# Two biases of a top-k softmax: a column on VectorE and a column on POOL, or both columns in one POOL product

## Chip, core and metric

The kernel runs on one core of a Trainium2 chip. The metric is the device time of one execution in microseconds (us), the median of several runs.

## What is computed

The reference is a chain of three layers. Of the first, the lines that matter here are these:

```python
top_k = 32
scores = scale * np.matmul(q, k.transpose(0, 1, 3, 2))
kth = np.partition(scores, -top_k, axis=-1)[..., -top_k:-top_k + 1]
scores = np.where(scores >= kth, scores, -1000000000.0)
scores = scores - np.max(scores, axis=-1, keepdims=True)
attn = np.exp(scores)
attn = attn / (np.sum(attn, axis=-1, keepdims=True) + 1e-09)
out = np.matmul(attn, v)
```

There are 4 batches, 8 heads, 576 positions and a head width of 64. Two mixture layers follow: `(x @ w_a) * (x @ w_b) @ w_out` on the 2304 tokens, then a router that picks one of 8 experts for each token, and that expert's two matrix products. Everything is float32.

## The kernel before

**The attention loop** runs over 144 rows. A "row" is 128 query positions against 576 keys, a tile `s` of 128x576. Rows are grouped in 32 parts; a part is a pair of heads with 256 or 320 of its query positions, and has 4 or 5 rows. One turn of the loop is one step. In a step, each row in flight is at another stage:

- Two steps ahead, TensorE (PE) makes the scores in PSUM (L359) and ScalarE (ACT) copies them to `s` in two halves (L360).
- `topk` (VectorE, DVE) finds the 32nd largest value of each line: four MAX8 (L380), each giving eight values of the tile `t` of 128x32, and three MATCH_REPLACE8 (L383) that blot out what was found. Each of the latter has a MATCH_VALUE_LOAD ahead of it, which reads the eight values of the MAX8. Two rows are interleaved: in one step DVE does the second half of the older row and the first half of the newer.
- Behind the older row's last MAX8 (and behind one MAX8 of the newer row) stands L385: the threshold, column 31 of `t`, times 2^66, into column 1 of a small tile `bi`.
- Two steps later, `softmax`: ACT makes a penalty, Relu(2^66 * (threshold - s)), with column 1 of `bi` as its bias (L392, called the Relu below). POOL then negates the row's largest value, column 0 of `t`, into column 0 of `bi` (L394) and subtracts the penalty from `s` (L395, the subtraction). At the start of the next step, ACT takes the exponential with column 0 of `bi` as its bias (L397).
- One step after that, PE transposes the result (L414), ACT copies it out (L417), and PE multiplies it by `v` (L453) at the end of a part.
- At a part's end `finish` runs on POOL: a product (L465) and a split in two halves (L216, L217). It is emitted at the end of a step.

Around this, POOL and ACT also convert the weights of the next layer (L531, L539, L541) up to about the fortieth row, and PE does the next layer's products between the rows (L672, L641), with POOL making two small products for each piece (L681, L628). The router of that layer has a short chain through all engines; in it ACT's L731 reads DVE's L729.

**What sets the order.** In this loop the order on PE, DVE, ACT and POOL is the order in which the code emits the instructions. Each engine works through its own list in order, and waits when an operand is not there. The DMA queue on SP is ordered by the scheduler. What follows the loop (from about 867 us) is the rest of the second layer and then the experts, and there only PE's order is written by hand.

The step's emission around the change is this: first the exponential of the row before, then a new `softmax` for row step-2, then sums of a part, then the step's share of `topk`; later, after the step's first transposes and scores, the Relu, and after the next transposes the subtraction.

```python
            with tc.high_priority(offset=FG):
                next(soft, None)
                soft = softmax(live[step - 2]) if 0 <= step - 2 < NRW else none
```

Of the kernel before, what the change touches and what calls it, by code (L numbers as in the profile page):

```python
# [10 lines left out]
F32 = mybir.dt.float32  # L11
# [6 lines left out]
OP = mybir.AluOpType  # L18
# [3 lines left out]
HUGE = float(2.0 ** 66)  # L22
# [60 lines left out]
def fused_kernel(  # L83
# [18 lines left out]
    pe, dve, act, pool, sp = nc.tensor, nc.vector, nc.scalar, nc.gpsimd, nc.sync  # L102
# [3 lines left out]
    P = 128  # L106
# [10 lines left out]
    cst = ctx.enter_context(tc.tile_pool(name="cst", bufs=1))  # L117
# [44 lines left out]
    dve.memset(eps, 1e-9)  # L162
    half = cst.tile([P, 1], F32, name="half")
    dve.memset(half, 0.5)

    tau1 = cst.tile([P, 1], F32, name="tau1")

# [28 lines left out]
    with ExitStack() as ph:  # L196
# [166 lines left out]
        def topk(t, fold):  # L363


            H2 = S // 2
            t.bi = wk.tile([P, 2], F32, name="bi", bufs=6)
            y = wk.tile([P, S], F32, name="y", bufs=YB)

            t8 = wk.tile([P, 32], F32, name="t8", bufs=6)  # L370
            t.top, t.thr = t8[:, 0:1], t8[:, 31:32]
            if fold:
                dve.tensor_tensor(y[:, :H2], t.s[:, :H2], t.s[:, H2:], op=OP.max)
                dve.tensor_tensor(y[:, H2:], t.s[:, :H2], t.s[:, H2:], op=OP.min)
                views = [(y[:, :H2], y[:, :H2])] * 2 + [(y, y)] * 2
            else:
                views = [(t.s, y)] + [(y, y)] * 3
            for r, (cur, rest) in enumerate(views):
                v = t8[:, r * 8 : r * 8 + 8]
                dve.max(v, cur)  # L380
                yield
                if r < 3:
                    dve.match_replace(out=rest, in_to_replace=v, in_values=cur, imm_value=LOWEST)  # L383
                    yield
            dve.tensor_scalar(t.bi[:, 1:2], t.thr, HUGE, None, op0=OP.mult)  # L385

        def softmax(t):
            t.w = wk.tile([P, S], F32, name="z", bufs=ZB)
            if PEN[t.n % len(PEN)]:
                dve.tensor_scalar(t.w, t.s, t.thr, HUGE, op0=OP.is_lt, op1=OP.mult)  # L390
            else:
                act.activation(t.w, t.s, AF.Relu, bias=t.bi[:, 1:2], scale=-HUGE)  # L392
            yield
            pool.tensor_scalar(t.bi[:, 0:1], t.top, -1.0, None, op0=OP.mult)  # L394
            pool.tensor_tensor(t.w, t.s, t.w, op=OP.subtract)  # L395
            yield
            act.activation(t.w, t.w, AF.Exp, bias=t.bi[:, 0:1], accum_out=t.o.sm[:, t.slot : t.slot + 1])  # L397
# [22 lines left out]
        def sums(o, add):  # L420
            sl = slice(0 if o.M else 4, 5 if o.tail else 4)
            if add:
                pool.tensor_scalar(o.rc[:, sl], o.sm[:, sl], 1e-9, None, op0=OP.add)
                return
            dve.reciprocal(o.rc[:, sl], o.rc[:, sl])
# [423 lines left out]
        soft = none  # L849
        for step in range(-AHEAD_L, NRW + TL + 5):  # L850
# [25 lines left out]
            with tc.high_priority(offset=FG):  # L876
                next(soft, None)
                soft = softmax(live[step - 2]) if 0 <= step - 2 < NRW else none
                for back in (3, 5):
                    j = step - back  # L880
                    if 0 <= j < NRW and rows[j][4] and (made[rows[j][:3]].n < F0 * NP) == (back == 3):
                        if back == 3:
                            sums(made[rows[j][:3]], True)
                        sums(made[rows[j][:3]], False)
                j = step - 4
                if 0 <= j < NRW and rows[j][4] and made[rows[j][:3]].n >= F0 * NP:
                    sums(made[rows[j][:3]], True)
                if 0 <= step < NRW:
                    cur = topk(live[step], FOLD[step % len(FOLD)])
                for _ in range(4):  # L890
                    next(thresholds[0], None)
                    next(cur, None)
                if step == NRW:
                    thresholds[0] = none
                elif 0 <= step < NRW:
                    thresholds[0] = cur
# [47 lines left out]
            if 0 <= i < NRW:  # L944
                next(tg, None)
                b, pr, part, first, last, kind, c, slot = rows[i]
                t = live.pop(i)
# [343 lines left out]
```

## Time and profile before

| what | us |
|---|---|
| median of 3 runs (1342.35 to 1346.2) | 1345.51 |
| the profiled execution, its own time | 1346.58 |
| its span, from the first to the last instruction | 1344.8 |
| PE busy in the span | 1158.5 |
| DVE busy | 925.3 |
| ACT busy | 796.6 |
| POOL busy | 768.4 |

Busy times are sums over the whole span, and the stages are not alike: DVE has almost nothing to do after the attention loop, and PE is busiest there. So the stage in which a change lies has to be read by itself. Waits are read from who released an instruction: an engine's line that is idle before an instruction names the instruction on another engine that ended the wait.

### The profile page before, as it was taken

To read this page: it belongs to the slowest core of one execution; us is meant where nothing else is said; L and a number is where in the kernel's file an instruction comes from. 1 tells how busy PE (TensorE), PEld (TensorE's weight loads), DVE (VectorE), ACT (ScalarE), POOL (GpSimd) and SP (SyncE) were. 2 spreads that over 40 slices of the span, in tenths; PEclk is the share of its full clock that TensorE was granted. 3 is DMA by queue.
4 is the path that set the end of the run, shared out by engine and by line. 5 is a ranking of instruction groups with operands and counts; after the bars stand their busy time and mean duration, and the time that the engine had idled before them with its cause. 6 is when DMAs were issued, how large, how long until landed. Compare 5 with 4: busy or idle time off the path is not lost. (4 is left out here: it accounts for less than half of the span.)

```text
span 1344.8 us, 22872 instructions
## 1 busy us (share of the span) xinstructions
PE 1158.5 (86%) x7720; PEld 987.7 (73%) x7721; DVE 925.3 (69%) x1990; ACT 796.6 (59%) x1917; POOL 768.4 (57%) x1196
## 2 busy tenths in 40 slices
PE   3566757778998989899989969899999989999996
PEld 2444645557786778778777858698898858888885
DVE  5999899997999999999989989412000135444440
ACT  4776666686767877777787767544332325444441
POOL 5765999875757776767677665654445422211100
PEclk9966878798999999999999999999999989999999
DMA  6333475446675467565666555589887135555520
GB/s 224 118 114 119 143 248 192 167 141 191 187 233 143 132 191 231 170 204 153 185 192 179 167 156 171 140 292 349 275 238 229 68 95 191 178 175 173 176 101 19
DMA packets 125707, 236.98 MB, mean 176 GB/s; under 512 B 22766, under 2 KB 71022, under 8 KB 125587
## 3 DMA queue, kind: packets, MB, share of 16 engines
q1 hardware_dynamic: 121426, 225.20, 53.4%
q0 software_dynamic: 4160, 10.29, 2.4%
q8 instruction: 62, 1.02, 0.3%
q14 instruction: 59, 0.48, 0.1%
HBM read 195.38 MB, written 40.85 MB: 176 GB/s over the span
## 5 line engine op out<-in xcount | busy, mean ns | idle before, releaser
L380 DVE MAX8 t<-y 128x8 f32<-128x576 f32 x432 | 311.7, 749 | 3.1
L395 POOL TENSOR_TENSOR z<-s,z 128x576 f32<-128x576 f32 x144 | 206.5, 1434 | 76.1 <-ACT z L392 75.7
L672 PE MATMUL ab<-xg,wab 128*128 128x256 f32 x1440 | 214.7, 294 | 12.7 <-POOL wab L541 8.2
L383 DVE MATCH_REPLACE8 y<-t,y 128x576 f32<-128x576 f32 x288 | 213.9, 743 | 0.0
L414 PE MATMUL tr<-ident,z 128*128 128x128 f32 x720 | 142.5, 300 | 73.3 <-ACT z L397 44.9
L672 PEld LDWEIGHTS ab<-xg,wab 128*128 128x128 f32 x1440 | 192.1, 196 | 17.7 <-POOL wab L541 9.0
L672 PE MATMUL ab<-raw,wab 128*128 128x256 f32 x1152 | 175.0, 295 | 14.4 <-DMA raw<-xl_d 6.7
L672 PEld LDWEIGHTS ab<-raw,wab 128*128 128x128 f32 x1152 | 154.8, 197 | 19.1 <-ACT gab L676 7.2
L397 ACT ACTIVATE z<-z,bi 128x576 f32<-128x576 f32 x144 | 111.8, 776 | 84.6 <-POOL z L395 84.1
L414 PEld LDWEIGHTS tr<-ident,z 128*128 128x128 f32 x720 | 93.8, 151 | 91.1 <-ACT z L397 49.1
L359 PE MATMUL tr<-kT,qT 128*128 128x288 f32 x512 | 133.3, 346 | 14.6 <-ACT s L360 9.3
L1046 POOL DMA_INDIRECT out_dram<-o,ids x24 | 23.7, 988 | 199.5 <-ACT o L1045 197.6
L641 PE MATMUL x<-wo,gh 128*128 128x512 f32 x432 | 137.7, 400 | 0.0
L417 ACT ACTIVATE wt<-tr 128x384 f32<-128x384 f32 (+2 forms) x320 | 125.8, 404 | 15.5 <-PE tr L414 15.3
L1074 PE MATMUL y<-u,hT 128*128 128x512 f32 (+1 forms) x528 | 128.1, 396 | 0.3 <-DVE hT L1179 0.3
L360 ACT ACTIVATE s<-tr 128x288 f32<-128x288 f32 x288 | 118.8, 412 | 16.2 <-PE tr L359 14.2
L997 DVE TENSOR_TENSOR u<-raw,u 128x1024 fp32r<-128x1024 f32 x64 | 76.7, 1229 | 72.5 <-ACT u L996 51.0
L681 POOL TENSOR_TENSOR gab<-gab 128x256 f32<-128x256 f32 x108 | 81.7, 756 | 65.0 <-ACT gab L676 58.8
L453 PE MATMUL tr<-wt,vs 128*64 128x256 f32 (+3 forms) x640 | 101.9, 458 | 12.7 <-ACT s L360 10.7
L628 POOL TENSOR_TENSOR gl<-gab,gh 128x256 fp32r<-128x256 f32 x108 | 81.7, 757 | 53.1 <-ACT gh L628 47.9
L392 ACT ACTIVATE z<-s,bi 128x576 f32<-128x576 f32 x144 | 111.8, 777 | 0.0
L380 DVE MAX8 t<-s 128x8 f32<-128x576 f32 x144 | 107.0, 743 | 4.6 <-ACT s L360 4.6
(171 smaller groups left out, 2168.9 us busy)
## 6 DMA issues: line engine op xcount, KB each, us to landing
wab<-wab_d SPq DMA_DIRECT2D x192, 512.0 KB, 4.5
raw<-in_moe_w_dram SPq DMA_DIRECT2D x28, 1024.0 KB, 5.2
wab_d<-wab SPq DMA_DIRECT2D x24, 512.0 KB, 4.5
kT_d<-kT SPq DMA_DIRECT2D x16, 576.0 KB, 3.2
kT<-kT_d SPq DMA_DIRECT2D x16, 576.0 KB, 6.7
vs<-in_v_dram SPq DMA_DIRECT2D x32, 256.0 KB, 2.8
raw<-in_moe_w_a_dram SPq DMA_DIRECT2D x12, 512.0 KB, 4.3
raw<-in_moe_w_b_dram SPq DMA_DIRECT2D x12, 512.0 KB
```

The source lines that it names most:

```text
L359: pe.matmul(p, l, r, start=(i == 0), stop=(i == len(terms) - 1))
L360: act.activation(t.s[:, cs], p, AF.Copy, scale=SCALE)
L380: dve.max(v, cur)
L383: dve.match_replace(out=rest, in_to_replace=v, in_values=cur, imm_value=LOWEST)
L392: act.activation(t.w, t.s, AF.Relu, bias=t.bi[:, 1:2], scale=-HUGE)
L395: pool.tensor_tensor(t.w, t.s, t.w, op=OP.subtract)
L397: act.activation(t.w, t.w, AF.Exp, bias=t.bi[:, 0:1], accum_out=t.o.sm[:, t.slot : t.slot + 1])
L414: pe.transpose(pt[:, i * P : (i + 1) * P], t.w[:, k0 : k0 + P], ident)
L417: act.activation(th[:, sl, w], pv[:, :, src], AF.Copy)
L641: pe.matmul(px[t], g[:, ts], wo[:, w, f], start=(f == 0 and i == 0), stop=(f == NF - 1 and i == 2))
L672: pe.matmul(p[:, i], wt[:, a, c, :], xg[x][:, c, :], start=(j == 0), stop=(j == len(terms) - 1))
L1074: pe.matmul(p[:m], (hi, lo)[a], u[:, b, f % 4, :], start=(f == 0 and i == 0), stop=(f == NF2 - 1 and i == 2))
```

## The change

The product of the threshold on DVE (L385) and the negation on POOL (L394) are taken out. In their place POOL makes one product of two columns: columns 0 and 31 of `t`, read with a stride of 31, times a constant tile `signs` that holds -1 and 2^66, into both columns of `bi`. It is emitted at the start of the step, as the first thing of `softmax`, and so ahead of the Relu instead of behind it. The tile `signs` is filled by two DVE memsets at the start of the kernel.

```diff
+    signs = cst.tile([P, 2], F32, name="signs")
+    dve.memset(signs[:, 0:1], -1.0)
+    dve.memset(signs[:, 1:2], HUGE)
...
             t8 = wk.tile([P, 32], F32, name="t8", bufs=6)
-            t.top, t.thr = t8[:, 0:1], t8[:, 31:32]
+            t.t8, t.thr = t8, t8[:, 31:32]
...
                     dve.match_replace(out=rest, in_to_replace=v, in_values=cur, imm_value=LOWEST)
                     yield
-            dve.tensor_scalar(t.bi[:, 1:2], t.thr, HUGE, None, op0=OP.mult)
 
         def softmax(t):
+            pool.tensor_tensor(t.bi, t.t8[:, 0:32:31], signs, op=OP.mult)
+            yield
             t.w = wk.tile([P, S], F32, name="z", bufs=ZB)
...
                 act.activation(t.w, t.s, AF.Relu, bias=t.bi[:, 1:2], scale=-HUGE)
             yield
-            pool.tensor_scalar(t.bi[:, 0:1], t.top, -1.0, None, op0=OP.mult)
             pool.tensor_tensor(t.w, t.s, t.w, op=OP.subtract)
...
                 next(soft, None)
                 soft = softmax(live[step - 2]) if 0 <= step - 2 < NRW else none
+                next(soft, None)
```

The change moves instructions on POOL. At the end of a part (here at the 96th row), POOL's list before has the part's `finish` (L465, L216, L217), then the negation and the subtraction:

```order
L628 TENSOR_TENSOR gl<-gab,gh 128x256
L394 TENSOR_SCALAR bi<-t_7368 128x1
L395 TENSOR_TENSOR z<-s,z 128x576
L465 TENSOR_TENSOR xsb<-xsb,xR 128x320
L216 TENSOR_SCALAR xh<-xsb 128x320
L217 TENSOR_TENSOR xR<-xsb,xh 128x320
L394 TENSOR_SCALAR bi<-t_7447 128x1
L395 TENSOR_TENSOR z<-s,z 128x576
```

In the changed kernel (lines are 4 to 6 higher: L391 is the new product, L399 the subtraction, L469, L220 and L221 the `finish`) the same place reads:

```order
L391 TENSOR_TENSOR bi<-t_7278,signs 128x2
L632 TENSOR_TENSOR gl<-gab,gh 128x256
L399 TENSOR_TENSOR z<-s,z 128x576
L469 TENSOR_TENSOR xsb<-xsb,xR 128x320
L220 TENSOR_SCALAR xh<-xsb 128x320
L221 TENSOR_TENSOR xR<-xsb,xh 128x320
L391 TENSOR_TENSOR bi<-t_7356,signs 128x2
L399 TENSOR_TENSOR z<-s,z 128x576
```

The new product stands where the step begins: in the upper row ahead of the step's other work (L632), in the lower one behind the whole `finish` of the step before; ACT's Relu, which reads it, is no longer free of POOL's list.

On DVE, before, a step of the loop at the same row reads as follows (`t_7447` is the older row's tile, `t_7544` the newer one's):

```order
L380 MAX t_7447<-y 128x8
L380 MAX t_7544<-s 128x8
L383 MATCH_REPLACE y<-t_7447,y 128x576
L383 MATCH_REPLACE y<-t_7544,s 128x576
L380 MAX t_7447<-y 128x8
L380 MAX t_7544<-y 128x8
L385 TENSOR_SCALAR bi<-t_7447 128x1
L383 MATCH_REPLACE y<-t_7544,y 128x576
```

and in the changed kernel (`t_7356` older, `t_7452` newer):

```order
L384 MAX t_7356<-y 128x8
L384 MAX t_7452<-s 128x8
L387 MATCH_REPLACE y<-t_7356,y 128x576
L387 MATCH_REPLACE y<-t_7452,s 128x576
L384 MAX t_7356<-y 128x8
L384 MAX t_7452<-y 128x8
L387 MATCH_REPLACE y<-t_7452,y 128x576
```

L385 stood between a MAX8 and the MATCH_REPLACE8 that reads that same MAX8's values; without it the two are neighbours. In the loop nothing else moves on PE, ACT or DVE. SP's queue has two weight loads one or two places later, and behind the loop a handful of ACT instructions and one matmul change places with a neighbour.

## Rows read from the trace of the kernel before

**Rows 1.** Stretch, length; busy us of PE, PEld, DVE, ACT, POOL; PE clock, DMA

```profile
150.00:359.00 209.00, 159.02 (x1051) 130.27 (x1051) 191.41 (x388) 144.53 (x349) 170.20 (x215) 0.85 0.57 188
359.00:867.00 508.00, 459.93 (x3412) 388.45 (x3411) 471.73 (x1079) 374.20 (x986) 352.56 (x592) 0.97 0.58 174
867.00:950.00 83.00, 79.52 (x561) 71.38 (x561) 12.25 (x23) 37.10 (x99) 44.47 (x87) 1.00 0.94 321
```

**Rows 2.** Waits of DVE from 150 to 867 us (total, times, longest)

```profile
DVE rc L425 <- POOL rc L423: 32.7, 12, 7.9
```

**Rows 3.** Waits of ACT from 150 to 867 us (total, times, longest)

```profile
ACT ex L731 <- DVE st L729: 19.2, 6, 5.9
```

**Rows 4.** Page, costliest groups: busy, mean ns of one, idle before

```profile
L392 ACT ACTIVATE z<-s,bi 128x576 f32<-128x576 f32 x144 | 111.8, 777 | 0.0
```

**Rows 5.** Timeline: first and last stretch that DVE holds (start, duration, wait before)

```profile
358.90 0.18 DVE L425 RECIPROCAL rc<-rc 128x4 f32<-128x4 f32 x1 [3.08 <-POOL rc L423]
...
400.17 0.39 ACT L731 ACTIVATE ex<-lg,st 128x8 f32<-128x8 f32 x1 [5.90 <-DVE st L729]
...
731.88 0.19 DVE L425 RECIPROCAL rc<-rc 128x5 f32<-128x5 f32 x1 [2.81 <-POOL rc L423]
...
773.16 0.39 ACT L731 ACTIVATE ex<-lg,st 128x8 f32<-128x8 f32 x1 [2.61 <-DVE st L729]
```

**Rows 6.** Timeline of DVE at the loop's first rows

```profile
22.46 0.74 DVE L380 MAX8 t<-s 128x8 f32<-128x576 f32 x1
23.23 0.09 DVE L383 MATCH_VALUE_LOAD y<-t,s 128x8 f32 x1
...
24.09 0.76 DVE L380 MAX8 t<-y 128x8 f32<-128x576 f32 x1
24.89 0.09 DVE L383 MATCH_VALUE_LOAD y<-t,y 128x8 f32 x1
...
28.52 1.41 DVE L380 MAX8 t<-y 128x8 f32<-128x576 f32 x2
29.85 0.14 DVE L385 TENSOR_SCALAR bi<-t 128x1 f32<-128x1 f32 x1
29.97 0.09 DVE L383 MATCH_VALUE_LOAD y<-t,y 128x8 f32 x1
```

**Rows 7.** Small instructions by line: duration min/median/max (ns), first and last start (us)

```profile
L385 DVE TENSOR_SCALAR bi<-t x144: 123/134/153, 29.9 to 856.6; 128x1 f32<-128x1 f32 x144
...
L394 POOL TENSOR_SCALAR bi<-t x144: 199/218/693, 33.6 to 864.8; 128x1 f32<-128x1 f32 x144
...
L710 POOL TENSOR_TENSOR st<-st,tau x18: 183/192/197, 290.3 to 1061.6; 128x1 f32<-128x1 f32 x18
```

**Rows 8.** Timeline of POOL, ACT and PE at one part's end

```profile
689.39 0.88 POOL L217 TENSOR_TENSOR xR<-xsb,xh 128x320 fp32r<-128x320 f32 x1
689.40 0.77 ACT L392 ACTIVATE z<-s,bi 128x576 f32<-128x576 f32 x1
...
690.07 0.38 ACT L417 ACTIVATE wt<-tr 128x256 f32<-128x256 f32 x1
...
690.24 0.21 POOL L394 TENSOR_SCALAR bi<-t 128x1 f32<-128x1 f32 x1
...
690.41 1.44 POOL L395 TENSOR_TENSOR z<-s,z 128x576 f32<-128x576 f32 x1
...
690.50 0.55 PE L414 MATMUL tr<-ident,z 128*128 128x128 f32 x3 [0.40 <-ACT wt L417]
```

**Rows 9.** Timeline: first and last Relu that precedes the product's new place

```profile
131.01 0.77 ACT L392 ACTIVATE z<-s,bi 128x576 f32<-128x576 f32 x1
...
863.38 0.81 ACT L392 ACTIVATE z<-s,bi 128x576 f32<-128x576 f32 x1
```

**Rows 10.** Timeline of POOL: a negation between work and an idle stretch ahead

```profile
609.93 0.20 POOL L747 TENSOR_TENSOR rk<-rk,base 128x8 f32<-128x8 f32 x1 [1.49 <-ACT rk L746]
...
613.14 0.26 POOL L394 TENSOR_SCALAR bi<-t 128x1 f32<-128x1 f32 x1
```

## The prediction

> **What bounds the kernel now.** I read the busy time by stretch first, then each engine's waits, then the timeline at a few places. The attention loop ends near 867 us; all the change's work lies before. There DVE looks like the bound: from 359 to 867 us it is busy 471.7 of 508 us, PE 459.9, ACT 374.2, POOL 352.6 [rows 1]. But two engines are nearly full, so the question is which of them the others wait for, and that changes along the loop. From 150 to 867 us DVE waits 32.7 us, 12 times, for POOL's sums at the end of a part [rows 2]: there DVE is ahead, and PE, ACT and POOL hold the time. ACT waits 19.2 us, 6 times, for DVE's router step L729 [rows 3]: there DVE is behind and holds it. The Relu itself never waits for DVE: its idle time is 0.0 [rows 4]. So a stretch from a wait of DVE to the next wait of ACT is DVE's, the rest belongs to the other three. From 359 us on, DVE holds four long stretches, the first from 358.90 to 400.17, the last from 731.88 to 773.16 us [rows 5]; between them are 507 to 538 and 550 to 648, in all 41 of the 144 rows. What follows counts an instant saved or lost only in the stretch whose holder saves or loses it.
>
> **L385 goes from DVE.** It takes 134 ns, 144 times, 19.3 us of busy time [rows 7]. What the engine gets back is another matter. With L385, two MAX8 start at 28.52 and the next MATCH_VALUE_LOAD starts at 29.97, 1.45 us later; the load starts 0.12 us after L385 [rows 6]. That 0.12 is the naive saving. Without L385 the load directly follows the MAX8 whose values it reads, and such neighbours are in the trace, at the first row: from 22.46 to 23.23 and from 24.09 to 24.89, 0.77 and 0.80 us from start to start, and the load begins 0.03 to 0.04 us after the MAX8's end [rows 6]. L385, by contrast, begins at 29.85, before the pair's end at 28.52 + 1.41 = 29.93 [rows 6]: instructions that don't need the last result overlap by 0.08 us. The pair with L385 spends 1.45 - 0.12 = 1.33 us up to L385's start, that is 0.67 us for each MAX8. A pair without L385 would take 0.67 + 0.77 to 0.67 + 0.80 = 1.44 to 1.47 us, against 1.45. L385 fills a gap in which DVE would wait for its own result. I take the saving as 0, with bounds from -0.01 to +0.02 us a row, on 41 rows -0.4 to +0.8 us.
>
> [...]
>
> **L394 becomes a product of two columns on POOL.** L394 takes 218 ns in the median; a POOL product of one column, L710, 192 [rows 7]. Two columns, one operand with a stride, are not in the trace. I take 0.20 us, near L710, with the range 0.19 to 0.22: 0.02 us less in a place, and the product lies on the path of POOL some 20 times: -0.4 us, from -0.6 to 0.
>
> **The product moves ahead to the start of the step.** On POOL this helps where the old place was between two pieces of work and the new one lies in idle time. At 613.14 the negation stood between a DMA and its subtraction, while POOL had idled 1.49 us up to 609.93 [rows 10]; the new place is ahead of that idle time. On the stretches that the other three hold I count 10 places of this kind, the one at 613 not among them: 10 x 0.20 = -2.0 us, from -2.6 to -1.0.
>
> **The Relu now waits for POOL.** This is the term that decides. It used to wait for DVE, which was done long before. Now it needs a product that stands in POOL's list behind all of the step before, and at a part's end that is the whole `finish`. At 689 us ACT begins the Relu at 689.40, while POOL is still in the split until 689.39 + 0.88 = 690.27 [rows 8]. Changed, the product runs from 690.27 to 690.47; with 0.05 us to start, the Relu begins at 690.52, 1.12 us later. Two things hang on it. POOL's subtraction, which follows directly, must wait for the Relu's end: 690.52 + 0.77 + 0.07 = 691.36 in place of 690.41, 0.95 us of idle POOL, and the exponential comes as much later. And behind the Relu in ACT's list stand L417 and L360, which empty PSUM: PE's transposes at 690.50 had already waited 0.40 us for L417 [rows 8] and now wait some 1.1 us more. So a three-engine chain POOL, ACT, POOL, ACT stands where the Relu used to run beside the split.
>
> I subtracted so at each row: product's earliest end, from the end of the instruction ahead of its new place, less the Relu's start. The Relu is late in 27 of 144 rows, the first at 131.01, the last at 863.38 us [rows 9]. Nearly all are ends of parts. In the other 117 POOL comes to the new place early enough. Where DVE holds the time, a late Relu costs nothing as long as it is less than the wait that ends the stretch (2.61 us at 773, 5.90 at 400) [rows 5]. In the weight conversion before 234 us, ACT waits for POOL just behind the Relu anyway, and I count nothing. What is left lies in stretches that PE, ACT and POOL hold: at 234 and 417 us 0.95 each, 492 and 498 together 0.5, 658 1.0, 689 and 715 1.1 each, 822 0.6, 841 0.95, and at 298, 800 and 863 0.3 each. The sum is +8.1 us. Its bounds: 4 if half of these are hidden by work that I did not see, 14 if the late Relus at 131 to 230 us (7.7 us in sum) count too.
>
> **The sum.** 0 - 0.4 - 2.0 + 8.1 = +5.7; I take off 0.7 for the three small ones at 0.3, of which some will hide, and have +5 us. The profiled execution took 1346.58, so 1351.6 there; it lies 1.07 above the median of the three, and against that the forecast is 1345.51 + 5 = 1350.5 us. What follows the loop shifts with it: the experts' weights begin to load when the loop's buffers are free, and from 867 to 950 us PE is busy 79.5 of 83 us and DMA 0.94 [rows 1], so I see no slack there that would take 5 us back. A measurement of this kernel can tell about 0.3%, 4.0 us, from no change, so the forecast lies just outside that.
>
> **Rivals.**
> - *DVE gets its 0.12 us back.* If the load did not wait for its MAX8, 41 rows x 0.12 = 4.9 us would go, and the time would be 1350.5 - 4.9 = 1345.6, no change. If DVE held the whole loop, 144 x 0.12 = 17.3 us less 3 us of late Relus: near 1331. It is for it that DVE is the busiest engine; against it are rows 6 and DVE's 32.7 us of waits, in which any gain would end. It becomes faster than 0.3% when it reaches some 75 rows: 75 x 0.12 = 9.0 us, less the 5. Chance 0.20, of which 0.12 for faster. [...]
> - *The late Relus are hidden.* ACT is idle for a quarter of the loop, and PE could make up for 1 us in its backlog of second-layer products. Then the terms left are -2.4, and the time is 1343 to 1348, no change. For it: PE idles 48 us between 359 and 867. Against it: PE works in order, and its transposes already waited for this very L417 [rows 8]. Chance 0.32.
> - *The late Relus cost everywhere.* The conversion's rows count and each loss pushes ACT and POOL past another: 14 to 20 us, 1357 to 1363. It takes POOL as the holder from 150 to 230 us, where it is nearly full. Chance 0.08.
> - *POOL waits for DVE.* The new product holds POOL's list until the row's last MAX8 is done. The threshold came at 29.9 us for the first row and at 856.6 for the last, POOL's negation at 33.6 and 864.8 [rows 7]: DVE is a step ahead or more. I find three rows in which POOL would arrive first, by 1.2 us at most. It costs under 1 us, unless DVE falls a whole step behind. Chance 0.04, in the slower part.
>
> **Chances.** The forecast itself, +4 to +9, has 0.36. Slower by over 0.3%: 0.36 + 0.08 + 0.04 of the last two rivals make 0.48. No change: 0.32 of the second rival and 0.08 of the first, 0.40. Faster: 0.12. The range goes from 1342, which takes in the hidden Relus and the partial gain of DVE, to 1357, where all late Relus begin to count.
>
> **What would show it.** DVE's step without L385: MAX8 to the load that follows should be 0.77 to 0.80 us, and DVE's busy time 19 us less, but the pitch of its rows the same. The Relu should show idle time in front of it, released by POOL's new product, 25 to 30 us in about 27 waits. The subtraction's wait for the Relu should grow by about 15 us. PE's waits for L417 should grow by some us between 650 and 720 us. The loop should end 5 us later, and the part behind it be as long as before. The prediction is wrong if DVE's rows come closer by 0.1 us each, or if the Relu waits as described and the loop ends no later.

## The result, and the profile after

| | kernel before | changed kernel |
|---|---|---|
| median of the runs | 1344.62 us (4 runs) | 1356.91 us (4 runs) |
| ratio, 95% interval | | 1.0078 [1.0061, 1.0095] |
| the profiled execution | 1346.58 | 1353.53 |

The change makes the kernel slower by 0.8%. The forecast was 1350.5 us in a range up to 1357. The profiled execution of the changed kernel was the fastest of its four, that of before was slower than each of its four, so the pair of traces differs by only 6.95 us.

The Relu is L397 now, and it has idle time in front of it, where [rows 4] showed 0.0. The page after, columns as in [rows 4]:

```profile
L397 ACT ACTIVATE z<-s,bi 128x576 f32<-128x576 f32 x144 | 111.7, 776 | 21.2 <-POOL bi L391 20.9
```

POOL's product L391, and who waited for it (all of the trace; duration min/median/max in ns, then us and times):

```profile
L391 POOL TENSOR_TENSOR bi<-t,signs x144: 182/193/1068, 29.5 to 869.9; 128x2 f32<-128x2 f32 x144
its engine sat idle before it (us, times) until:
  DVE t L384: 3.7, 3
who waited for it (us, times):
  ACT z L397: 20.9, 22
```

Waits from 150 to 867 us in the changed kernel (total, times, longest), those of the loop's three-engine chain and those that answer to [rows 2, 3]:

```profile
POOL z L399 <- ACT z L397: 77.8, 63, 5.5
ACT z L401 <- POOL z L399: 62.6, 58, 3.3
PE tr L418 <- ACT wt L421: 36.5, 26, 5.5
DVE rc L429 <- POOL rc L427: 35.6, 14, 7.8
ACT z L397 <- POOL bi L391: 19.1, 20, 2.4
ACT ex L735 <- DVE st L733: 15.2, 6, 5.9
```

The same for the kernel before:

```profile
ACT z L397 <- POOL z L395: 80.3, 69, 4.0
POOL z L395 <- ACT z L392: 60.0, 43, 5.1
...
PE tr L414 <- ACT wt L417: 26.4, 26, 4.5
```

ACT's waits hardly change in sum: what it now waits ahead of the Relu (19.1) it waits less ahead of the exponential (62.6 for 80.3). But POOL's wait for the Relu grows by 17.8 us and PE's wait for the copies behind it by 10.1. DVE waits 2.9 us more for POOL and ACT 4.0 less for DVE: DVE is ahead more often than before, as it should be when the other three lose time.

A place like that of [rows 8], row 111 of the changed kernel (start, duration, idle time before and its releaser):

```profile
694.79 0.87 POOL L221 TENSOR_TENSOR xR<-xsb,xh 128x320 fp32r<-128x320 f32 x1
695.62 0.19 POOL L391 TENSOR_TENSOR bi<-t,signs 128x2 f32<-128x2 f32 x1
...
694.50 0.40 ACT L364 ACTIVATE s<-tr 128x288 f32<-128x288 f32 x1
695.85 0.78 ACT L397 ACTIVATE z<-s,bi 128x576 f32<-128x576 f32 x1 [0.94 <-POOL bi L391]
```

The product stands behind the split, and the Relu starts 0.23 us after the product's start, 0.04 behind its end (0.05 taken). POOL's subtraction follows at 696.70, 0.07 behind the Relu's end, as taken. The last Relu starts 6.8 us later than before (870.13 against 863.38), the span is 7.0 longer (1351.8 against 1344.8): nearly all is lost by the loop's end, and the part behind it gives nothing back.

### The profile page after: what moved, and what is told of

Same layout as the page of the kernel before. It is cut to its first block, busy times and chain, and to the rows that moved or that the text cites. A ratio compares the mean times of both kernels' runs of the same rounds, so it can differ in the third digit from the quotient of the medians.

```text
span 1351.8 us, 22729 instructions
## 1 busy us (share of the span) xinstructions
PE 1161.4 (86%) x7720; PEld 988.8 (73%) x7721; DVE 922.0 (68%) x1848; ACT 800.6 (59%) x1917; POOL 762.5 (56%) x1196
## 5 line engine op out<-in xcount | busy, mean ns | idle before, releaser
L399 POOL TENSOR_TENSOR z<-s,z 128x576 f32<-128x576 f32 x144 | 205.6, 1427 | 94.9 <-ACT z L397 94.6
L1051 POOL DMA_INDIRECT out_dram<-o,ids x24 | 23.9, 997 | 200.9 <-ACT o L1050 195.1
L397 ACT ACTIVATE z<-s,bi 128x576 f32<-128x576 f32 x144 | 111.7, 776 | 21.2 <-POOL bi L391 20.9
L457 PE MATMUL tr<-wt,vs 128*64 128x256 f32 (+3 forms) x640 | 104.8, 468 | 11.0 <-ACT s L364 9.1
L1079 PEld LDWEIGHTS y<-u,hT 128*128 128x128 f32 (+1 forms) x528 | 89.7, 173 | 28.1 <-DVE hT L1184 0.5
```

Of the source, the lines that this page charges most:

```text
L1079: pe.matmul(p[:m], (hi, lo)[a], u[:, b, f % 4, :], start=(f == 0 and i == 0), stop=(f == NF2 - 1 and i == 2))
```

## Experiments

Three theories stood against each other. **Late Relu**: the loss is the Relu's wait for a product that stands behind `finish`. **DVE's gap**: L385 costs nothing where it stood, so its removal saves nothing (against it: 0.12 us a row come back, and the late Relus cost even more than the result shows). **Accounting**: a late Relu costs its own length in a stretch that PE, ACT and POOL hold, and nothing in one that DVE holds.

### The changed kernel again

> The changed kernel once more, as the mark for the runs beside it. All theories: about 1.0078 of the kernel before (1.006 to 1.0095). In its trace the Relu should again wait some 20 times for POOL's new product.

1354.43 us, ratio 1.0066 [1.0051, 1.0081]. The Relu waits 21.4 us in 25 rows. By this set the loss is 8.9 us, by the first 10.5.

### The product ahead of the finish

```diff
-                next(soft, None)
-                soft = softmax(live[step - 2]) if 0 <= step - 2 < NRW else none
                 next(soft, None)
+                soft = coming_soft
...
+            with tc.high_priority(offset=FG):
+                coming_soft = softmax(live[step - 1]) if 0 <= step - 1 < NRW else none
+                next(coming_soft, None)
             run_due()
```

The product is emitted at the end of the step before, ahead of `run_due()`, which emits `finish`.

> The new two-column product is emitted at the end of the step before, ahead of a part's finish (product and split on POOL), instead of behind it; all else as in the changed kernel. Theory 'late Relu' (the loss is the Relu that waits behind finish): the Relu's wait for POOL falls from 20 us to under 5 us and the loss goes: 0.997 to 1.002 of the kernel before. Theory 'product itself' (the two-column form, the lost overlap on VectorE or the order behind the loop costs the time): stays at 1.005 to 1.009.

1345.37 us, ratio 0.9996 [0.9981, 1.0012]. The page:

```profile
L397 ACT ACTIVATE z<-s,bi 128x576 f32<-128x576 f32 x144 | 111.8, 776 | 4.8 <-POOL bi L391 4.7
```

The same product, ahead of `finish` in POOL's list instead of behind it, and the loss is gone with 16 of the 21 us of waits. So it is the wait, and not the product.

### The negation early, L385 kept

```diff
+            pool.tensor_scalar(t.bi[:, 0:1], t.top, -1.0, None, op0=OP.mult)
+            yield
             t.w = wk.tile([P, S], F32, name="z", bufs=ZB)
...
-            pool.tensor_scalar(t.bi[:, 0:1], t.top, -1.0, None, op0=OP.mult)
             pool.tensor_tensor(t.w, t.s, t.w, op=OP.subtract)
...
+                next(soft, None)
```

> The kernel before with only the place of POOL's negation changed: it stands at the start of the step, where the changed kernel has its product, and the threshold's bias stays on DVE, so the Relu waits for POOL in no row. By the theory, in which the late Relu is the whole loss, the time is that of before or up to 3 us less (the gain of the earlier place that the prediction counted at 2.0 us): 1340 to 1345, ratio 0.998 to 1.001. If the place itself costs (a product that holds up POOL's list until a row's last MAX8, or the shift of all that follows), the ratio is above 1.003 with no wait of the Relu.

1342.38 us, ratio 0.9981 [0.9967, 0.9994], and the Relu's idle time is 0.0. POOL's instruction stands where the changed kernel has its product; since nothing on ACT waits for it, the place brings 2.6 us (0.8 to 4.4). The sum had 2.0.

### L385 kept beside the product

```diff
+            dve.tensor_scalar(t.bi3[:, 2:3], t.thr, HUGE, None, op0=OP.mult)
```

> The changed kernel with VectorE's one-column product put back into a third column that nobody reads, so that VectorE has its old list again. Theory 'gap' (the removed instruction only filled the wait of the next load for the MAX8): same time as the changed kernel within 0.2%, row pitch on VectorE 5.08 us in both. Theory 'VectorE got 0.12 us a row back': slower than the changed kernel by 41 x 0.12 = 5 us, 0.37%.

1351.87 us, ratio 1.0048 [1.0034, 1.0061]. With the instruction put back on DVE the kernel is not slower than without it (1.0066 beside it); if its removal had saved 4.9 us, this version would have lost them.

### The kernel before without L385, twice

```diff
-            dve.tensor_scalar(t.bi[:, 1:2], t.thr, HUGE, None, op0=OP.mult)
-                act.activation(t.w, t.s, AF.Relu, bias=t.bi[:, 1:2], scale=-HUGE)
+                act.activation(t.w, t.s, AF.Relu, bias=half, scale=-HUGE)
```

and the second time `bias=t.thr, scale=-1.0` in place of `bias=half, scale=-HUGE`.

> The kernel before without the threshold's bias on DVE: the Relu takes a constant column in its place, so the threshold is left out of the result. POOL's negation stays where it was, no wait is added, so only the saving on DVE is left. If the instruction lies in a gap in which DVE waits for its own MAX8, the step from a last MAX8 to the load stays 0.777 us, the pitch of the rows 5.085 us, and the time is that of before within 0.2%, 1343 to 1349. If DVE gets 0.12 us back in each row, the pitch falls to 4.97 us and the time by 5 us on the 41 rows that DVE holds, to 1341 to 1343, or by up to 17 us if it holds more.

> The kernel before without the threshold's bias on DVE, once more: the Relu now takes the threshold itself, with a scale of -1 in place of the large factor, so the mask only pushes the scores below the threshold down by their distance to it and does not cut them off. The amounts of work in the tail should so stay near those of before, and the whole time can be compared. If the instruction lies in a gap of DVE, the time is that of before within 0.2%, 1341 to 1346, and MAX8 to load stays 0.777 us. If the loop really gains from it, as the loop's end of the first attempt (5 us earlier than in the profile of before) could mean, it is 1337 to 1340, ratio 0.994 to 0.998.

1885.23 and 2140.47 us: a miss of mine. The other scores send the tokens to other experts, and products for the surplus tokens run behind everything (L1232, which has no instruction in the trace of before, 704 in the second). The whole times tell nothing. The loop can still be read. In the second run its Relus start within 0.2 us of those of before from row 5 to row 108, and the last 0.7 us earlier; in the first 1 to 3 us earlier in most rows and 5.4 at the end. Both leave out the same instruction, so its removal doesn't explain the 5.4. TensorE's granted clock differs by about as much: the time lost to it from 230 to 870 us (one less the granted clock, times 4 us, summed over stretches of 4 us) is 23.9 us in the first trace, 29.1 in the second and 25.6 in that of before. DVE in the second, without L385:

```profile
303.66 1.41 DVE L380 MAX8 t<-y 128x8 f32<-128x576 f32 x2
305.11 0.09 DVE L383 MATCH_VALUE_LOAD y<-t,y 128x8 f32 x1
```

1.45 us from the pair's start to the load, as with L385 in [rows 6]. Over the trace, a last MAX8 that is directly followed by its load takes 776.5 ns in the mean up to the load in the changed kernel (146 cases), and 776.6 with L385 between them in the kernel before. The pitch of DVE's rows is 5.087 us in the median in both, and in the two runs here.

### Both columns in one product on DVE

```diff
+            dve.tensor_tensor(t.bi, t.t8[:, 0:32:31], signs, op=OP.mult)
...
-            pool.tensor_tensor(t.bi, t.t8[:, 0:32:31], signs, op=OP.mult)
-            yield
```

> The mirror of the change: the two-column product stands on VectorE where the one-column product stood, POOL has neither. Theory 'gap': VectorE's rows keep their pitch of 5.08 us, POOL loses 144 negations of 0.22 us, some 20 of them on its path, no Relu waits for POOL: faster than the kernel before by 2 to 6 us, 0.995 to 0.999. Theory 'VectorE bounds the loop': 1.000 or slower.

1353.31 us, ratio 1.0046 [1.0033, 1.0060]: a miss, slower than before, though only two rows wait for it. DVE and POOL at its worst instance:

```profile
409.65 1.41 DVE L384 MAX8 t<-y 128x8 f32<-128x576 f32 x2
410.97 2.18 DVE L389 TENSOR_TENSOR bi<-t,signs 128x2 f32<-128x2 f32 x1
413.08 0.08 DVE L387 MATCH_VALUE_LOAD y<-t,y 128x8 f32 x1
...
410.59 1.10 POOL L759 DMA_INDIRECT ids_d<-tk,ds  x1 [0.56 <-POOL ds L758]
411.71 1.42 POOL L398 TENSOR_TENSOR z<-s,z 128x576 f32<-128x576 f32 x1
```

Two elements a partition take 2.18 us, and end where POOL's subtraction ends (411.71 + 1.42 = 413.13). The instruction takes 130/147/2184 ns (min, median, max) and 359 in the mean. In 57 of 144 rows it is over 250 ns, and each of these ends within 0.09 us of the end of an instruction on POOL, in 56 with a product or subtraction of two tiles beside it. Of the 87 short ones 26 overlap such a neighbour too, but all save one only at its start or in its last stretch, ending within 0.1 us behind it. DVE's busy time is 953.3 us against 925.3, and the median pitch of its rows 5.29 us against 5.09. What ties its end to that of POOL's instruction is not shown.

### Both on DVE, one input each

```diff
             dve.tensor_scalar(t.bi[:, 1:2], t.thr, HUGE, None, op0=OP.mult)
+            dve.tensor_scalar(t.bi[:, 0:1], t.top, -1.0, None, op0=OP.mult)
...
-            pool.tensor_scalar(t.bi[:, 0:1], t.top, -1.0, None, op0=OP.mult)
```

> The kernel before, with the negation taken from POOL to DVE as an instruction of its own behind the threshold's bias, so both are instructions with one input and POOL has none of the two. If the loss of the two-column product on DVE came from its two inputs (mean 359 ns, up to 2.2 us, beside POOL's work), the two here take 120 to 160 ns each whatever POOL does, the row pitch of DVE grows by 0 to 0.08 us, which is 0 to 3.3 us on the 41 rows that DVE holds, and POOL loses 144 x 0.22 = 31 us of work: 1343 to 1349, ratio 0.997 to 1.001. If that loss came from any second small instruction on DVE, the time is like that of the product, 1351 to 1355, ratio above 1.003, and the instructions here show long durations too.

> The version with both biases on DVE as two instructions of one input, which was ahead of the kernel before at 0.9969 [0.9947, 0.9990], on another set of runs. If the gain is real, 0.995 to 0.999 again; if it was a scatter of the first set, 0.999 to 1.002. MAX8 to load should stay 0.777 us with both instructions between them.

1339.51 us, ratio 0.9969 [0.9947, 0.9990], and again 1341.05 us, 0.9965 [0.9952, 0.9977]: faster than both kernels. Its DVE (of the second run):

```profile
303.82 1.41 DVE L380 MAX8 t<-y 128x8 f32<-128x576 f32 x2
305.15 0.13 DVE L385 TENSOR_SCALAR bi<-t 128x1 f32<-128x1 f32 x1
305.20 0.14 DVE L386 TENSOR_SCALAR bi<-t 128x1 f32<-128x1 f32 x1
305.26 0.09 DVE L383 MATCH_VALUE_LOAD y<-t,y 128x8 f32 x1
```

Two small instructions stand between the MAX8 and the load, and the load still comes 1.44 us after the pair's start. No duration of either exceeds 153 ns, whatever POOL does. They differ from the product in columns and stride too, so that its second input makes it wait is a guess of mine: no run here separates it. The gap holds both, POOL is rid of 144 instructions, and ACT waits for DVE in 2 rows (3.2 us).

### Which late rows cost

The product ahead of the finish again, but for twelve rows (60, 106, 111, 116 and others: those that the prediction counted), or for all but these.

```diff
+        COUNTED = (29, 39, 60, 74, 75, 106, 111, 116, 131, 135, 139, 143)
...
+                if step - 2 in COUNTED:
+                    next(soft, None)
...
-                next(coming_soft, None)
+                if step - 1 not in COUNTED:
+                    next(coming_soft, None)
```

> The changed kernel, with POOL's product ahead of the finish in all rows but the twelve for which the prediction counted a loss (29, 39, 60, 74, 75, 106, 111, 116, 131, 135, 139, 143); those keep it at the start of their own step. The rows whose late Relu the prediction called hidden or absorbed are so made punctual. By the accounting of the prediction nearly the whole loss is in these twelve: about 7 us above the version with the product ahead of the finish everywhere (1345.4), 1351 to 1353, ratio to before 1.004 to 1.006. By the rival, in which the rows that were called absorbed carry most of it, 1346 to 1349, ratio 1.000 to 1.003. About 8 to 9 us of waits of the Relu for POOL are left in either case.

> The other half of the same split: the product stands ahead of the finish in the twelve counted rows alone, and at the start of its own step in the other 132. Left late are then the rows that the prediction took to be covered: 17 to 28 by the weight conversion, 49, 55, 65, 85 to 87, 96, 101 and 121 by DVE, which was read as the one that holds the time there. By the accounting of the prediction these cost nothing: 1344 to 1347, ratio 0.998 to 1.002. By the rival they cost 4 us or more: 1349 to 1353, ratio 1.003 to 1.006. About 12 us of the Relu's waits are left in either case. If the losses of the two halves add up to some 9 us, what the changed kernel loses in all, the split is clean; if they add up to more or less, late rows also act on each other.

Late in the twelve: 1353.23 us, ratio 1.0071 [1.0052, 1.0090]. Late in the others: 1346.46, 1.0020 [1.0004, 1.0035]. Against the 0.9996 of the product ahead everywhere, the twelve cost 0.75% or 10.1 us, the others 0.24% or 3.2 us, each give or take 3. The rows were picked right. The 7.4 us that the sum had for the twelve lie inside the interval, near its lower end.

Row by row the traces show where. The table gives how much the Relus fall behind those of the version without late rows from one row to the next shown (difference of the Relus' starts):

| rows from, to | late within | counted, us | twelve late | gap filled (next run) |
|---|---|---|---|---|
| 57, 63 | 60 | 0.95 | 2.4 | 0.9 |
| 72, 80 | 74, 75 | 0.5 | 0.2 | 2.2 |
| 103, 108 | 106 | 1.0 | 1.1 | 0.8 |
| 110, 112 | 111 | 1.1 | 0.9 | 0.9 |
| 112, 115 | | 0 | 0.1 | 1.5 |
| 115, 118 | 116 | 1.1 | 2.8 | 0.4 |
| 126, 134 | 131 | 0.3 | 1.1 | 1.2 |
| 134, 143 | 135, 139, 143 | 1.85 | 1.5 | 1.6 |

In this trace two places hold most of the excess, 60 and 116. At row 60, PE in the version without late rows, then in the one with twelve:

```profile
419.56 0.55 PE L418 MATMUL tr<-ident,z 128*128 128x128 f32 x3 [0.41 <-ACT wt L421]
...
420.69 1.12 PE L676 MATMUL ab<-xg,wab 128*128 128x256 f32 x8
```

```profile
420.33 0.55 PE L418 MATMUL tr<-ident,z 128*128 128x128 f32 x3 [1.43 <-ACT wt L421]
...
421.54 1.91 PE L676 MATMUL ab<-xg,wab 128*128 128x256 f32 x8
```

PE waits 1.43 us in place of 0.41, and then the same eight products take 1.91 us in place of 1.12, with no idle time between them. The stretches of 4 us (columns as in [rows 1]; the granted clock is the third number from the end), without late rows, then with twelve:

```profile
420.00:424.00 4.00, 4.00 (x36) 4.00 (x36) 3.93 (x8) 3.74 (x12) 1.77 (x3) 1.00 0.35 101
```

```profile
420.00:424.00 4.00, 3.67 (x21) 3.67 (x22) 3.93 (x10) 3.75 (x13) 1.69 (x3) 0.66 0.10 35
...
722.00:726.00 4.00, 3.38 (x16) 3.38 (x17) 3.93 (x14) 3.55 (x13) 1.92 (x5) 0.50 0.25 65
726.00:730.00 4.00, 4.00 (x21) 3.67 (x21) 3.93 (x9) 2.73 (x7) 2.82 (x5) 0.69 0.76 230
```

Behind the gap at row 60 the granted clock reads 0.66 in place of 1.00. The same happens at row 116, where PE's wait grew from 0.40 to 1.44 us: 0.50 and 0.69 in the two stretches behind it, where it is 1.00 in both without late rows.

In the other half, the Relus are 3.8 us behind at row 90, 6.0 at row 103 (96 and 101 are late between them) and 3.5 at row 108: what these two rows cost is given back. There DVE holds the time, and the accounting is right. What stays is lost ahead of row 65 (0.5 us behind at row 64, 3.4 at row 65), which starts at 446.88 us without late rows, outside of DVE's stretches; my expectation put the row among DVE's, wrongly. But it is not a late Relu that loses it: the Relus of rows 56 to 64 wait for nothing, and that of row 65 for only 0.27 us. PE's wait ahead of it is the same in both traces, and only the clock behind it differs. Without late rows, then with the others late:

```profile
439.35 4.44 PE L457 MATMUL tr<-wt,vs 128*64 128x320 f32 x20 [3.07 <-ACT s L364]
```

```profile
439.89 5.79 PE L457 MATMUL tr<-wt,vs 128*64 128x320 f32 x20 [3.08 <-ACT s L364]
```

```profile
442.00:446.00 4.00, 4.00 (x36) 2.58 (x32) 2.86 (x6) 3.41 (x9) 2.36 (x4) 0.98 0.22 66
```

```profile
442.00:446.00 4.00, 4.00 (x18) 1.39 (x16) 2.98 (x6) 2.49 (x7) 1.96 (x2) 0.50 0.00 0
```

So the clock also differs from trace to trace where no Relu is late.

### The gap filled

To tell the clock from the late Relu: the twelve late rows as above, but at 60 and 116 PE's transposes ahead of the gap are issued three times. The order of everything else is the same.

```diff
+        FILLED = (61, 62, 117, 118)
...
-                pe.transpose(pt[:, c * P : (c + 1) * P], x.rearrange("p a d -> p (a d)"), identr)
+                for _ in range(3 if now[0] in FILLED else 1):
+                    pe.transpose(pt[:, c * P : (c + 1) * P], x.rearrange("p a d -> p (a d)"), identr)
```

> The version with twelve late rows, and in two of them (60 and 116) the transposes that stand in TensorE's list just ahead of the gap are issued three times instead of once, on the same data: 12 transposes more at each place, which at 0.11 us each fill most of the 1.4 us in which TensorE waits there behind the late Relu. The late Relus stay, and the order of everything else is the same. In the trace of the version with twelve late rows the granted clock fell behind these two gaps (0.66 from 420 to 424 us, 0.50 and 0.69 from 722 to 730), and the rows came 2.4 and 2.9 us later, of which the late Relu itself is 0.95. If the idle TensorE is what brings the lower clock and the rest of the delay, the clock stays near 1.00 behind both places, each costs 1.0 to 1.3 us, and the whole is some 3 us faster: 1349 to 1351, ratio about 1.004 to 1.006. If the clock falls all the same, or the delay comes from something else in the late row, the time is 1353 or, with the added work, a little more, ratio 1.007 or above.

1351.36 us, ratio 1.0062 [1.0042, 1.0081]; against 1.0071 the whole times don't tell the two apart. The two places do:

```profile
416.26 1.70 PE L307 MATMUL tr<-identr,qs 128*128 128x128 f32 x18 [0.73 <-POOL xh L220]
418.46 0.55 PE L419 MATMUL tr<-ident,z 128*128 128x128 f32 x3 [0.50 <-ACT wt L422]
...
419.58 1.12 PE L677 MATMUL ab<-xg,wab 128*128 128x256 f32 x8
```

```profile
420.00:424.00 4.00, 4.00 (x33) 3.87 (x33) 4.00 (x8) 4.00 (x12) 1.58 (x2) 1.00 0.47 136
...
722.00:726.00 4.00, 4.00 (x31) 3.71 (x30) 3.97 (x10) 3.86 (x13) 2.19 (x8) 1.00 0.56 181
```

The Relus are late as before (0.94 and 0.93 us), PE does 12 transposes more at each place, the clock stays at 1.00, the eight products take 1.12 us, and the rows fall behind by 0.9 and 0.4 us instead of 2.4 and 2.8 (table). So there the excess came with the lower clock. But in this run the clock fell behind two other late rows instead: 0.66 from 490 us, 0.74 from 694, where the table has 2.2 and 1.5 us.

That PE's idle time brings the lower clock, and that the added work kept it away, is not shown. Five traces have a late Relu at rows 60 and 116:

| trace | PE's wait at 60, 116, us | granted clock behind it | rows 57 to 63, 115 to 118 fall behind, us |
|---|---|---|---|
| changed kernel | 1.44, 1.44 | falls, stays | 2.4, 0.4 |
| changed kernel again | 0.98, 1.44 | stays, falls | 0.9, 1.5 |
| L385 kept unread | 1.45, 1.45 | stays, falls | 0.9, 1.5 |
| twelve late | 1.43, 1.44 | falls, falls | 2.4, 2.8 |
| gap filled | 0.50, 0.49 | stays, stays | 0.9, 0.4 |

Where the clock fell, the rows lost 1.5 to 2.8 us; where it stayed, 0.4 to 0.9, with the gap filled or not. A lower clock does not always cost: behind row 106 it fell in both traces of the table before this one (0.71 and 0.58 from 662 us), and the rows lost only 1.1 and 0.8 us. With L385 kept, row 60 has the whole gap and the clock stays at 1.00:

```profile
418.44 0.55 PE L420 MATMUL tr<-ident,z 128*128 128x128 f32 x3 [1.45 <-ACT wt L423]
...
419.56 1.12 PE L678 MATMUL ab<-xg,wab 128*128 128x256 f32 x8
```

```profile
418.00:422.00 4.00, 3.56 (x30) 3.57 (x31) 3.96 (x10) 3.86 (x14) 1.58 (x3) 1.00 0.18 49
422.00:426.00 4.00, 4.00 (x31) 3.74 (x30) 3.97 (x10) 4.00 (x11) 2.47 (x4) 1.00 0.71 253
```

In the kernel before it fell behind row 116 (0.62 from 718 us) with no late Relu at all.

## Why the prediction was right, and where it fell short

**L385's removal saves nothing: right.** Its pitch per row stayed (5.087 us in the median), and MAX8 to load is 776.5 ns. One sign was wrong: DVE's busy time fell by 3.3 us (925.3 to 922.0) and not by 19. Most of L385 lay over its neighbours' ends ([rows 6]: it begins 0.08 us before the MAX8's end), and busy time counts such an overlap once. One instruction less in this gap changes nothing (776.6 ns with L385), and one more changes nothing either: a pair's start to the load is 1.44 us without any and with two.

**POOL's product: right.** 193 ns in the median (0.20 taken), the two longest 705 and 1068.

**The earlier place brings 2.0 us: right for the negation.** 2.6 us (0.8 to 4.4) with the negation alone. For the product it is not clear: ahead of the finish, and so early too, it brings 0.5 us (from 2.6 gained to 1.6 lost).

**The late Relu: right in mechanism and place, small in size.** 25 late rows (27 forecast) with 21.2 us of waits (25 to 30 forecast), the subtraction's wait 17.8 us longer (15 forecast). The term was +8.1, less 0.7. Measured against the version with the product ahead of the finish, beside it in the same set, it is 9.4 us, give or take 2.9. Worked out as the second set's loss of 8.9 plus the 2.6 that the place brings, it is 11.5, give or take 2.7. Both lie inside the bounds of 4 to 14, and only the second is clear of the 7.4. The step that came out small is "0.95 us of idle POOL, and the exponential comes as much later": the sum counted for each late row its own delay. That fits where the granted clock stays (0.9 us at row 60; 0.4 at row 116, for the 1.1 counted), but in some traces the clock fell behind these two rows, and then they lost 1.5 to 2.8 us. [rows 8] showed that PE's transposes had already waited 0.40 us for L417, and the prediction wrote that they would wait some 1.1 more, but gave neither that nor the clock a price. PE's waits for these copies grew by 10.1 us over the loop, though by only 1.7 between 650 and 720 us, where the prediction looked for it.

How much of the whole loss is the clock's can only be estimated, from the mean granted clock of every execution (one less that clock, times the span). The changed kernel loses 92 and 93 us to it in its two sets, the kernel before 86 beside the second; the twelve late rows 91 for 85. But with the gap filled it is 85 for 84, and that kernel still loses 0.62%; with L385 kept and all late Relus 87 for 86, and a loss of 0.48%. Over 157 executions of all versions but the two without L385, each compared with the others of its own version and set, 1 us more of lost clock goes with 0.2 us more time. So my estimate for the clock's part is 1 to 3 us of the 9 to 10; most of the loss is the wait.

**Where luck comes in.** The first set's median, 1356.91, lies 0.1 us inside the range. On the 1345.51 that the forecast started from, the two ratios would give 1356.0 and 1354.4: the loss is about double the forecast 5 us, at or just above the top of the +4 to +9 that had the chance of 0.36.

**The holder of the time: right where it was tested.** Rows 96 and 101 gave their delay back in DVE's stretch. Row 65 lies outside of these stretches and was not counted; what was lost ahead of it in the one trace was the clock.

**The rivals.** DVE's 0.12 us did not come back; the late Relus were not hidden; POOL did wait for DVE three times (3.7 us), as counted, with a longest wait of more than the 1.2 us forecast.

**Open:** why the version with L385 kept unread is a little faster than the changed kernel (1.0048 against 1.0066, the intervals overlap). In its trace the time lost to the clock from 230 to 870 us is 25.6 us in place of 30.6 with the same 21 us of late Relus, which would fit, but no run tested it. What makes the clock fall behind one gap of 1.4 us and not behind the next is open as well.

## What to carry to other kernels

Before moving an operand's producer to another engine, look at what stands ahead of it in that engine's list at the worst step: here a 0.2 us product cost 9 to 10 us behind a `finish`, and nothing ahead of it. A small instruction between a producer and its reader on one engine can be free, as L385 was (776.6 ns from MAX8 to load with it, 776.5 without): look at the gap that remains without it, and try more of the small work there. Here two instructions of one input fitted (153 ns at most), and a product of two tiles did not (up to 2184 ns). And where TensorE gets a longer gap, read the granted clock behind it in several traces of the same kernel: behind the same wait of 1.44 us at row 116 of the changed kernel it stayed at 1.00 in one trace and fell to 0.72, over 4 us, in the other.

## What the runs showed of the hardware that I had not expected

- A VectorE product of two tiles, 128x2, took 130 ns or up to 2184 ns, ending with POOL's instruction beside it; one-input instructions of 128x1 never took more than 153 ns.
- Two one-input instructions of 0.13 and 0.14 us fitted into the gap between a MAX8 and the load that reads it: from the pair's start to the load it took 1.44 us with both, as in the changed kernel with neither.
- Behind the same TensorE wait of 1.4 us, at the same rows of the same loop, the granted clock fell in some traces (to 0.50 to 0.79 in the lowest stretch of 4 us) and stayed at 1.00 in others. Where it fell, eight products took 1.91 us instead of 1.12 (row 60), and the rows lost 1.1 to 2.4 us more than where it stayed.
